# Half slots store each column half by itself, and the split of w1's last row moves to the next slot's head

## The chip, the cores and the metric

One core of a Trainium2 chip runs the whole program. The metric is the device time of one execution in microseconds. The core's engines are PE (matrix products, with PEld loading weights), DVE (vector), ACT (scalar), POOL (GpSimd) and SP (which issues most loads). Each engine takes its instructions in order from a queue of its own. Loads and stores with an index per row (indirect DMAs) are issued by POOL.

## The reference

Attention with a sigmoid in place of the softmax, then a mixture of eight experts in which each token goes to the one expert with the largest gate:

```python
scores = scale * q @ k.T - log(S)          # 8 batches, 12 heads, S = 448, head_dim = 64
attn   = sigmoid(scores);  x = attn @ v    # x: 3584 tokens x 768
logits = x @ w_gate                        # 8 experts
e_idx  = argmax(logits);  gate_w = softmax(logits)[e_idx];  eom = sigmoid(x @ w_output_gate)
for e in range(8):
    h = relu(x[mask_e] @ w1[e])            # 768 -> 1024
    out[mask_e] = gate_w * eom[:, e] * (h @ w2[e])    # 1024 -> 768
```

## The kernel before

Attention fills the first part of the span. `route` finds each token's expert and scatters one line per token (row numbers, token number, factor) into a list in DRAM, ordered by expert. The experts' part then works in slots. A slot takes up to 256 tokens of one expert: POOL gathers their rows of x (`gather`, L501), DVE transposes them (`turn_x`, L558), ACT and DVE split x and the weights into a rounded high part and the remaining low part (`split`, L532 and L533; pairs of w1 rows in `split_w1`, L536 and L539), PE forms both layers from the parts, ACT scales the result into `y` (`layer2_out`, L621), and POOL scatters y's rows into `out` (L623). The tokens left over per expert go into wide slots (192 tokens, whose last 64 go out by `layer2_q`, L677) and half slots (128 tokens). How many there are depends on the data: the last loops are nested `tc.If` blocks, one block a slot. In the profiled execution three wide slots and two half slots run; the half slots are the last 45 us.

A half slot `half_slot(j, y)` works for itself and prepares its successor, whether or not one will run (there are eight blocks): it asks for the successor's w1 and w2 (issued only if the expert changes), gathers the successor's rows, waits for POOL to drain (L717), forms its layer 1, then turns the successor's x, splits w1's first four rows and x (`split_w1(0)`, `split_x`, `split_w1(1)`), and, while PE forms layer 2, row 4 of w1 (`split_w1_row(4)`). Then each column half n of the output is evicted by ACT. After that row 5 of w1 is split. The order of the work on each engine is the order of the program (a manual schedule). What the engines wait for is worked out by the framework from the regions that instructions write and read; the text writes no wait by hand.

`out` is written by every slot. A slot's store is an indirect DMA with one index per token, of 768 words a row. `layer2_q` sees `out` as twice as many rows of 384 words, with its own index list `ltq` (twice the token's number, plus the half). `finish` stores a slot's second half late, inside the next slot; in half slot 0 it is the last wide slot's. `y` is one of two buffers, and half slot j uses `ys[j % 2]`. The half slots' index and factor are in `ltb`, eight lists of 128 tokens, filled once in `spread_rest`'s neighbourhood early in the experts' part. `ltb` lies in the tail of the buffer `gl1`, of which the last sixteen words are free.

Of the kernel before, what the change touches and what calls it, by code (L numbers as in the profile page):

```python
# [14 lines left out]
ALU = mybir.AluOpType  # L15
# [5 lines left out]
B, H, S, D = 8, 12, 448, 64  # L21
NPAIR = H // 2
E = 8
DM = H * D
DF = 1024
NT = B * S
# [28 lines left out]
def r32(ap):  # L55
    return ap.bitcast(F32)


class Kernel:
# [78 lines left out]
    def constants(self):  # L138
        nc = self.nc
# [21 lines left out]
            t, pattern=pattern, base=base, channel_multiplier=0, allow_small_or_imprecise_dtypes=True)  # L161
# [40 lines left out]
        own = gl[1].bitcast(I32)  # L202
# [11 lines left out]
        self.ltb = own[:, a:a + 2 * E].rearrange("p (k h w) -> p k h w", h=1, w=2)  # L214
        a += 2 * E
        self.at = own[0:GT, a:a + LGR + 1]
        self.route_tiles()

    def row_words(self):
# [260 lines left out]
    def spread_rest(self):  # L480
        g = self.nc.gpsimd
        a = EARLY + LATE_F
        for i in range(4):
            r, q = slice(32 * i, 32 * i + 32), slice(32 * (i % 2), 32 * (i % 2) + 32)
            own = self.lts[q, a:, 1]
            g.tensor_scalar(self.ltq[r, :, 0], own[:, :, 0], 2.0, float(i // 2), ALU.mult, ALU.add)
            g.tensor_copy(r32(self.ltq[r, :, 1]), r32(own[:, :, 1]))

    def load_rows(self, i):
        self.nc.gpsimd.indirect_dma_start(  # L490
            out=self.lr[i], out_offset=None, in_=self.lst.rearrange("(r t) w -> r (t w)", t=32),
            in_offset=bass.IndirectOffsetOnAxis(ap=self.at[:, i:i + 1], axis=0))
# [122 lines left out]
    def finish(self):  # L615
        self.layer2_out(self.psy[2], dict(lt=self.due.unsqueeze(1)), 0, 1, self.ys[1])

    def layer2_out(self, ps, s, t, n, y):
        nc = self.nc
        c = slice(384 * n, 384 * n + 384)  # L620
        nc.scalar.activation(y[:, c], ps, AF.Copy, scale=r32(s["lt"][:, t, 1:2]))  # L621
        if n == 1:
            nc.gpsimd.indirect_dma_start(  # L623
                out=self.out, out_offset=bass.IndirectOffsetOnAxis(ap=s["lt"][:, t, 0:1], axis=0),
                in_=y, in_offset=None, bounds_check=NT - 1, oob_is_err=False)
# [43 lines left out]
    def layer2_q(self, s, y):  # L669
        nc = self.nc  # L670
        ps = self.psy[0]
        for f in range(8):
            for n in range(2):
                nc.tensor.matmul(ps[64 * n:64 * n + 64], self.hq[:, f], self.w2r[:, f, 384 * n:384 * n + 384],
                                 start=(f == 0), stop=(f == 7))
        nc.scalar.activation(y[:, 0:384], ps, AF.Copy, scale=r32(s["lq"][:, 1:2]))
        nc.gpsimd.indirect_dma_start(  # L677
            out=self.out.rearrange("t (n c) -> (t n) c", n=2),
            out_offset=bass.IndirectOffsetOnAxis(ap=s["lq"][:, 0:1], axis=0),
            in_=y[:, 0:384], in_offset=None, bounds_check=2 * NT - 1, oob_is_err=False)  # L680

    def wide_slot(self, j):
        cur = self.wide_lists(j)
# [25 lines left out]
    def half_slot(self, j, y):  # L709
        nc = self.nc  # L710
        nx = None
        if j + 1 < E:
            nx = self.load_slot(self.tab_b, j + 1, self.half_lists(j + 1))
        if j:
            if nx is not None:
                self.gather(self.half_lists(j + 1))
            nc.gpsimd.drain()  # L717
        (wh, wl), (xh, xl), (hh, hl) = self.w1s, self.xs, self.hs

        def turn(n):  # L720
            ps = self.take("x", self.psx).rearrange("p a (b t) -> p (a b) t", b=2)
            for i in range(4):
                nc.tensor.transpose(ps[:, i], self.hb[:, 128 * (4 * n + i):128 * (4 * n + i + 1)], self.ident)  # L723
            fs = slice(4 * n, 4 * n + 4)
            self.split(ps, hh[:, fs, 0:HS], hl[:, fs, 0:HS])

        w2 = [self.w2_rows(k) for k in range(4)]
        low = lambda k: nc.vector.tensor_tensor(w2[k][2], w2[k][0], r32(w2[k][1]), ALU.subtract)
        for n in range(2):
            c = slice(512 * n, 512 * n + 512)  # L730
            ps = self.take("h", self.psh)
            for d in range(6):
                if n == 1 and d == 3:
                    turn(0)
                    low(2)
                    nc.scalar.copy(w2[3][1], w2[3][0])
                    low(3)
                nc.tensor.matmul(ps, xh[:, d, 0:HS], wh[d][:, c], start=(d == 0), stop=False)  # L738
                nc.tensor.matmul(ps, xh[:, d, 0:HS], wl[d][:, c], start=False, stop=False)  # L739
                nc.tensor.matmul(ps, xl[:, d, 0:HS], wh[d][:, c], start=False, stop=(d == 5))  # L740
            if n == 0:
                self.split_w2(0)
                self.split_w2(1)
            nc.scalar.activation(self.hb[:, c], ps, AF.Relu)
            if n == 0:
                nc.scalar.copy(w2[2][1], w2[2][0])
        cur = dict(lt=self.ltb[:, j])
        pss = self.psy[0:2]
        self.layer2_mm(pss[0], 0, 0, range(2))
        turn(1)  # L750
        if j == 0:
            self.finish()
        if nx is not None:
            self.turn_x(nx)
            self.split_w1(0)
            for k in range(3):
                self.split_x(nx, k)
            self.split_w1(1)
        self.layer2_mm(pss[0], 0, 0, range(2, 4))
        self.layer2_mm(pss[1], 0, 1, range(4))  # L760
        self.load_w2(nx)
        if nx is not None:
            self.split_w1_row(4)
        for n in range(2):
            self.layer2_mm(pss[n], 0, n, range(4, 8))
            self.layer2_out(pss[n], cur, 0, n, y)
        if nx is not None:
            self.split_w1_row(5)

    def attention(self, pool, rows):  # L770
        nc = self.nc
# [276 lines left out]
```

## Time and profile before

| | |
|---|---|
| time, median of 3 runs | 783.53 us (783.46 to 785.43) |
| the profiled execution | 785.01 us, of which the span from first to last instruction is 783.3 us |
| granted clock of TensorE, mean | 0.996 |
| busy: PE, DVE, ACT, POOL | 98%, 64%, 62%, 45% of the span |
| half slot 0, layer 1 on PE begins | 738.76 us |
| half slot 1, layer 1 on PE begins | 758.16 us |
| PE's last matmul ends | 775.98 us |

Times in the views are microseconds from the span's start. The busy shares are averages over the whole span; the change touches the last 45 us and an early line of the list's arithmetic. In a timeline a row is an instruction or a run of equal ones; the bracket at its end gives the engine's idle time before it and what ended that. A DMA row on POOL is the time in which POOL writes the transfer's descriptors; the landing, when the data is there, comes later.

### The profile page before, as it was taken

To read this page: it belongs to the slowest core of one execution; us is meant where nothing else is said; L and a number is where in the kernel's file an instruction comes from. 1 tells how busy PE (TensorE), PEld (TensorE's weight loads), DVE (VectorE), ACT (ScalarE), POOL (GpSimd) and SP (SyncE) were. 2 spreads that over 40 slices of the span, in tenths; PEclk is the share of its full clock that TensorE was granted. 3 is DMA by queue.
4 is the path that set the end of the run, shared out by engine and by line. 5 is a ranking of instruction groups with operands and counts; after the bars stand their busy time and mean duration, and the time that the engine had idled before them with its cause. 6 is when DMAs were issued, how large, how long until landed. Compare 5 with 4: busy or idle time off the path is not lost. (4 is left out here: it accounts for less than half of the span.)

```text
span 783.3 us, 15087 instructions
## 1 busy us (share of the span) xinstructions
PE 767.6 (98%) x5724; PEld 561.6 (72%) x5724; DVE 497.8 (64%) x800; ACT 488.1 (62%) x662; POOL 353.9 (45%) x464
## 2 busy tenths in 40 slices
PE   9999999999999999999999999999999999999896
PEld 4333433333443369899999989999899999889685
DVE  2334444443456768876786576858577685787677
ACT  5666666666668757565675565746556474675585
POOL 4003301230331676778895667255372643633522
PEclk9999999999999999999999999999999999999999
DMA  6352544445258550147666497511156655856771
GB/s 252 142 212 91 195 165 173 159 143 213 81 204 303 191 184 12 53 176 238 232 201 249 160 343 280 182 51 42 40 223 204 259 158 210 315 212 237 278 307 46
DMA packets 37616, 145.23 MB, mean 185 GB/s; under 512 B 5639, under 2 KB 7791, under 8 KB 33552
## 3 DMA queue, kind: packets, MB, share of 16 engines
q1 hardware_dynamic: 27696, 119.56, 42.6%
q0 software_dynamic: 9824, 24.46, 9.3%
q8 instruction: 51, 0.84, 0.4%
q14 instruction: 45, 0.37, 0.2%
HBM read 152.61 MB, written 23.05 MB: 224 GB/s over the span
## 5 line engine op out<-in xcount | busy, mean ns | idle before, releaser
L800 ACT ACTIVATE a<-ps,bias_s 128x896 f32<-128x896 f32 x168 | 169.1, 1008 | 96.6 <-PE ps L798 96.6
L576 PE MATMUL ps<-rounded 128*128 128x512 f32 (+1 forms) x672 | 225.9, 386 | 1.7 <-PEq L990 1.2
L501 POOL DMA_INDIRECT plain<-x_dram,lxs x122 | 181.9, 1491 | 65.2 <-issue 40.5
L577 PE MATMUL ps<-rounded 128*128 128x256 f32 (+1 forms) x672 | 184.1, 274 | 1.4 <-DVE rounded L539 1.2
L798 PE MATMUL ps<-kqv 64*64 64x448 f32 x1344 | 157.9, 541 | 0.4 <-ACT a L800 0.4
L807 PE MATMUL ps<-a,kqv 64*64 64x448 f32 x1344 | 156.8, 536 | 0.0
L601 PE MATMUL ps<-w2h,h 128*128 128x384 f32 x432 | 144.9, 335 | 0.0
L533 DVE TENSOR_TENSOR w2l<-plain,w2h 128x1536 fp32r<-128x1536 f32 x60 | 105.2, 1757 | 62.0 <-ACT w2h L532 61.4
L602 PE MATMUL ps<-w2l,h 128*128 128x384 f32 x432 | 144.4, 334 | 0.0
L603 PE MATMUL ps<-w2h,h 128*128 128x384 f32 x432 | 144.4, 334 | 0.0
L576 PEld LDWEIGHTS ps<-rounded 128*128 128x128 f32 x672 | 125.8, 187 | 25.0 <-issue 3.0
L577 PEld LDWEIGHTS ps<-rounded 128*128 128x128 f32 x672 | 127.2, 189 | 2.3 <-DVE rounded L539 2.0
L807 PEld LDWEIGHTS ps<-a,kqv 64*64 64x64 f32 x1344 | 51.6, 133 | 75.3 <-issue 74.2
L539 DVE TENSOR_TENSOR rounded<-plain,rounded 128x2048 fp32r<-128x2048 f32 x46 | 103.3, 2284 | 1.8 <-ACT rounded L536 1.8
L798 PEld LDWEIGHTS ps<-kqv 64*64 64x64 f32 x1344 | 48.7, 133 | 74.0 <-issue 60.7
L532 ACT CAST w2h<-plain 128x1536 fp32r<-128x1536 f32 x60 | 88.1, 1472 | 19.3 <-PEq L995 6.3
L584 ACT COPY gl<-ps 128x256 f32<-128x256 f32 (+1 forms) x112 | 40.3, 360 | 93.9 <-PE ps L577 87.0
L536 ACT CAST rounded<-plain 128x2048 fp32r<-128x2048 f32 x46 | 87.3, 1903 | 0.0
L601 PEld LDWEIGHTS ps<-w2h,h 128*128 128x128 f32 x432 | 81.1, 188 | 2.3 <-issue 1.8
L602 PEld LDWEIGHTS ps<-w2l,h 128*128 128x128 f32 x432 | 81.1, 188 | 0.1
L603 PEld LDWEIGHTS ps<-w2h,h 128*128 128x128 f32 x432 | 81.1, 188 | 0.0
L623 POOL DMA_INDIRECT out<-y,due x11 | 18.3, 1666 | 117.6 <-ACT gl L584 92.4
(209 smaller groups left out, 716.5 us busy)
## 6 DMA issues: line engine op xcount, KB each, us to landing
plain<-w SPq DMA_DIRECT2D x68, 768.0 KB
plain<-w SPq DMA_DIRECT2D x48, 1024.0 KB
kqv<-kqv SPq DMA_DIRECT2D x23, 1344.0 KB
x_dram<-xt SPq DMA_DIRECT2D x8, 1344.0 KB
plain<-w SPq DMA_DIRECT2D x6, 512.0 KB
plain<-x_dram,lxs POOLq DMA_INDIRECT x122, 5.0
kqv<-kqv SPq DMA_DIRECT2D x1, 896.0 KB
lst<-plain POOLq DMA_DIRECT2D x1, 726.0 KB, 7.2
```

The lines of the kernel that those rows point to most:

```text
L501: self.nc.gpsimd.indirect_dma_start(out=s["xg"][:, g], out_offset=None, in_=x4, in_offset=bass.IndirectOffsetOnAxis(ap=s["lx"][:, g:g + 1] ...
L532: self.nc.scalar.copy(hi, raw)
L533: self.nc.vector.tensor_tensor(lo, raw, r32(hi), ALU.subtract)
L539: self.nc.vector.tensor_tensor(self.w1p[1][k], self.w1r[:, 2 * k:2 * k + 2], r32(self.w1p[0][k]), ALU.subtract)
L576: nc.tensor.matmul(out, wh[d][:, c], both, start=(d == 0), stop=False)
L577: nc.tensor.matmul(ps[:, 0:n], wl[d][:, c], self.xc[:, d, 0, 0:n], start=False, stop=(d == 5))
L601: nc.tensor.matmul(ps, hh[:, f, tk], wh, start=(f == 0), stop=False)
L602: nc.tensor.matmul(ps, hh[:, f, tk], wl, start=False, stop=False)
L603: nc.tensor.matmul(ps, hl[:, f, tk], wh, start=False, stop=(f == 7))
L798: nc.tensor.matmul(ps[half[h], j, 0:S], kg[half[j], e, 0, o:o + 64], kg[half[j], e, 1], start=True, stop=True)
L800: nc.scalar.activation(at[u % 4], ps[:, :, 0:S], AF.Sigmoid, bias=self.bias_s, scale=1.0 / math.sqrt(D))
L807: nc.tensor.matmul(self.ps_o[e][h][half[j], 0:S], v[half[h], 6 if i == 3 else 3 * e + c, j], a[half[h], j], start=(i in ((0, 3 if h else 4 ...
```

## The change

`spread_rest` computes a second index list `ltc` for the half slots, with two entries per token: twice the token's number, plus 0 and plus 1. `layer2_out` takes it as `rows` from `half_slot` and then stores each column half by itself, right behind its eviction, by the helper `store_part` that `layer2_q` uses too. So a half slot issues two indirect stores of 384-word rows instead of one of 768-word rows. And `split_w1_row(5)` is no longer the last thing of a half slot but the first thing of the next one, inside its block.

```diff
@@ (the lists)
+        self.ltc = own[:, S - 2 * E:].rearrange("p (k w) -> p k w", w=2)
@@ spread_rest
+        for n in range(2):
+            g.tensor_scalar(self.ltc[:, :, n:n + 1], self.ltb[:, :, :, 0], 2.0, float(n), ALU.mult, ALU.add)
@@ layer2_out
-    def layer2_out(self, ps, s, t, n, y):
+    def layer2_out(self, ps, s, t, n, y, rows=None):
         nc = self.nc
         c = slice(384 * n, 384 * n + 384)
         nc.scalar.activation(y[:, c], ps, AF.Copy, scale=r32(s["lt"][:, t, 1:2]))
-        if n == 1:
+        if rows is not None:
+            self.store_part(rows[:, n:n + 1], y[:, c])
+        elif n == 1:
             nc.gpsimd.indirect_dma_start(
                 out=self.out, out_offset=bass.IndirectOffsetOnAxis(ap=s["lt"][:, t, 0:1], axis=0),
                 in_=y, in_offset=None, bounds_check=NT - 1, oob_is_err=False)
@@ layer2_q, and the new helper
-        nc.gpsimd.indirect_dma_start(
+        self.store_part(s["lq"][:, 0:1], y[:, 0:384])
+
+    def store_part(self, rows, y):
+        self.nc.gpsimd.indirect_dma_start(
             out=self.out.rearrange("t (n c) -> (t n) c", n=2),
-            out_offset=bass.IndirectOffsetOnAxis(ap=s["lq"][:, 0:1], axis=0),
-            in_=y[:, 0:384], in_offset=None, bounds_check=2 * NT - 1, oob_is_err=False)
+            out_offset=bass.IndirectOffsetOnAxis(ap=rows, axis=0),
+            in_=y, in_offset=None, bounds_check=2 * NT - 1, oob_is_err=False)
@@ half_slot, head
         nx = None
+        if j:
+            self.split_w1_row(5)
         if j + 1 < E:
             nx = self.load_slot(self.tab_b, j + 1, self.half_lists(j + 1))
@@ half_slot, end
         for n in range(2):
             self.layer2_mm(pss[n], 0, n, range(4, 8))
-            self.layer2_out(pss[n], cur, 0, n, y)
-        if nx is not None:
-            self.split_w1_row(5)
+            self.layer2_out(pss[n], cur, 0, n, y, self.ltc[:, j])
```

## Rows read from the trace of the kernel before

**Rows 1.** Windows: busy us of PE, PEld, DVE, ACT, POOL; clock, DMA share, GB/s.

```profile
776.00:778.00 2.00, 0.00 (x0) 0.00 (x0) 2.00 (x2) 1.83 (x3) 0.83 (x1) 1.00 0.05 16
781.50:783.30 1.80, 0.00 (x0) 0.00 (x0) 0.00 (x0) 0.00 (x0) 0.00 (x0) 0.50 0.00 0
```

**Rows 2.** Source view of L1003 from 781 us: duration (ns), first and last start.

```profile
L1003 POOLq INC_SWDGE_SEM  x1: 188/188/188, 781.5 to 781.5; - x1
```

**Rows 3.** Timeline of POOL, half slots: start, us, what, idle time before and releaser.

```profile
752.45 0.99 POOL L623 DMA_INDIRECT out<-y,due  x1 [14.79 <-ACT y L621]
760.45 1.03 POOL L623 DMA_INDIRECT out<-y,gl  x1 [7.01 <-ACT rounded L532]
761.79 2.51 POOL L501 DMA_INDIRECT plain<-x_dram,gl  x1 [0.30 <-DVE rounded L533]
764.61 1.35 POOL L501 DMA_INDIRECT plain<-x_dram,gl  x1 [0.30 <-issue]
766.25 0.95 POOL L501 DMA_INDIRECT plain<-x_dram,gl  x1 [0.30 <-issue]
767.51 1.46 POOL L501 DMA_INDIRECT plain<-x_dram,gl  x1 [0.30 <-issue]
777.17 1.17 POOL L623 DMA_INDIRECT out<-y,gl  x1 [8.21 <-ACT y L621]
```

**Rows 4.** Timeline of ACT, the half slots.

```profile
757.54 0.58 ACT L621 ACTIVATE y<-ps,gl 128x384 f32<-128x384 f32 x1
...
772.16 1.02 ACT L532 CAST rounded<-plain 128x256 fp32r<-128x256 f32 x3 [1.01 <-DVE plain L558]
...
775.85 1.04 ACT L621 ACTIVATE y<-ps,gl 128x384 f32<-128x384 f32 x2
776.78 1.04 ACT L532 CAST rounded<-plain 128x1024 fp32r<-128x1024 f32 x1
```

**Rows 5.** Timeline of DVE, the half slots.

```profile
759.42 2.35 DVE L533 TENSOR_TENSOR rounded<-plain,rounded 128x1024 fp32r<-128x1024 f32 x2
761.69 3.42 DVE L533 TENSOR_TENSOR w2l<-plain,w2h 128x1536 fp32r<-128x1536 f32 x2
...
766.39 3.41 DVE L728 TENSOR_TENSOR w2l<-plain,w2h 128x1536 fp32r<-128x1536 f32 x2
...
771.09 0.98 DVE L558 STREAM_TRANSPOSE plain<-plain 128x768 f32<-128x768 f32 x1 [0.69 <-DMA plain<-x_dram,gl]
...
775.17 2.28 DVE L539 TENSOR_TENSOR rounded<-plain,rounded 128x2048 fp32r<-128x2048 f32 x1
777.37 2.35 DVE L533 TENSOR_TENSOR rounded<-plain,rounded 128x1024 fp32r<-128x1024 f32 x2
```

**Rows 6.** Source view of L623, 752 to 753 us: a queue's wait (ns), landing.

```profile
L623 POOLq EVENT_SEMAPHORE  x1: 7428/7428/7428, 752.3 to 752.3; - x1
...
DMA to landing us min/median/max: 7.2/7.2/7.2
```

**Rows 7.** Timeline of POOL in a full slot: two stores in a row.

```profile
330.72 1.10 POOL L623 DMA_INDIRECT out<-y,lts  x1 [0.30 <-issue]
335.26 1.14 POOL L623 DMA_INDIRECT out<-y,lts  x1 [3.44 <-ACT h L589]
```

**Rows 8.** Source view of L623, 330 to 331 us: landing of the first.

```profile
DMA to landing us min/median/max: 3.7/3.7/3.7
```

**Rows 9.** Waits of the whole span: the scatters into the list.

```profile
POOL lst L317 <- DMA lst<-meta,posi: 41.3, 22, 5.3
```

**Rows 10.** Source view of L623 over the whole span: landing of its stores.

```profile
DMA to landing us min/median/max: 3.0/4.3/8.0
```

**Rows 11.** DMA view, 758 to 766 us: rate in 40 slices.

```profile
GB/s 277 200 169 61 77 61 31 15 15 0 0 0 0 0 0 0 0 0 0 0 461 399 338 369 384 0 0 0 0 0 0 82 0 0 0 230 154 38 31 31
```

**Rows 12.** Source view of L677, whole span: landing, rows of 384 words.

```profile
DMA to landing us min/median/max: 3.7/6.0/6.1
```

**Rows 13.** Source view of L486: index arithmetic on POOL, ns min/median/max.

```profile
L486 POOL TENSOR_SCALAR gl<-lts x4: 199/200/208, 417.4 to 418.7; 32x10 int32<-32x10 int32 x4
```

## The prediction

> **What bounds the kernel now.** I read the page first: PE is busy 98% of the span, so time can only be won or lost where PE is not the last to finish. The windows of the tail show such a place: from 776 us on PE does nothing, while DVE, ACT and POOL still work, and in the last 1.8 us no engine is busy [rows 1]. The span ends 1.8 us after POOL's queue gets past 781.5, and what it stands behind there is the landing of the last store: issued at 777.17, landed 4.3 us later [rows 2, 3]. So the end is set by one store, plus 1.8 us of closing work.
>
> Then I followed that store back through the timelines, each row giving what ended the idle time before it. The store starts 0.28 us after ACT's second eviction (776.89) [rows 3, 4]. The evictions start at 775.85, behind casts for a successor slot that never runs, and these start at 772.16, when DVE has turned x, for which DVE waited until 771.09 on the last gather [rows 4, 5]. That gather was issued at 767.51 as the last of four, the first at 761.79, right behind the store of half slot 0 at 760.45 [rows 3]. So the critical chain of the last slot begins at POOL in slot 0: store, four gathers, turn, casts, evictions, store, end. Whatever is put on POOL between 760 and 768 us, or between two stores, can reach the end.
>
> One wait in that chain decides the rest. The store at 760.45 was not waiting for its data: its first half had been evicted from 757.54 to 758.12 and its second shortly after [rows 4]. POOL's queue sat 7.43 us in one wait from 752.3, that is until 759.7; the store before it (`finish`, issued at 752.45, another y buffer) took 7.2 us to land, until 759.65, and 0.8 us later the next store started [rows 3, 6]. What these two share is `out`. The same stands at the two stores of a full slot: the first, issued at 330.72, lands 3.7 us later at 334.42, the second starts at 335.26, 0.84 us after that [rows 7, 8]. The scatters into the list behave so too: 22 times one waited for the landing of the one before, 41.3 us in all [rows 9]. I read this as a rule of this program: a store into `out` starts about 0.8 us after the previous store into `out` has landed.
>
> **Part 1, the index list.** Two POOL instructions in `spread_rest`, at most 0.2 us each by their neighbour of the same kind [rows 13], 340 us before the half slots and behind nothing that PE waits for: 0. Without that cover 0.4 us.
>
> **Part 2, two stores in half slot 0.** The first half (A) still starts at 760.45, since it waits for `finish`, not for its data. It lands 2.5 to 3.0 us after its start: the shortest landing of a whole store is 3.0 [rows 10], and in the store at 760.45 the bytes move for 1.0 us (five slices at 338 to 461 GB/s) [rows 11], half of which may go with half the bytes. Among gathers and weight loads the stores of 384-word rows took 3.7 to 6.1 [rows 12]; the half slots issue few loads, so I keep 3.7 as the slow end. So A lands at 763.0 to 763.5 and the second half (B) starts 0.8 us later, at 763.8 to 764.3. B is new on POOL, and the four gathers are queued behind it.
>
> What B takes depends on DVE. A gather that starts while DVE works on a pair of SBUF tensors ends only 0.85 to 0.9 us after that DVE instruction's end: the one at 761.79 took 2.51 and ended at 764.30, 0.9 after the first of the two w2 instructions (761.69, 3.42 for both) must have ended; the one at 764.61 ended 0.85 after the second; the store at 777.17 ended at 778.34, 0.89 after the DVE row that ended at 777.45. The gather at 766.25, started just before a DVE pair, took 0.95 [rows 3, 5]. So B, started inside the second w2 instruction (to 765.11), ends at 765.96. The gathers follow 0.30 us apart: the first from 766.26 to 767.21, the second 767.51 to 768.97 (where the fourth stood before), the third from 769.27, held until DVE's pair ends at 769.80, to 770.66, the fourth from 770.96 to 771.91, now without a DVE instruction in the way. Before, the turn began 2.12 us after the fourth gather's issue ended (768.97 to 771.09), so it now begins at 774.03: later by 2.9. If B is not held, the row of gathers comes one place earlier and the shift is 1.7; if B misses its place by a gather, 4.2. I take 2.9, since B's start falls well inside that DVE instruction.
>
> By the Trainium skill, SBUF — State Buffer, section "SBUF: two separate sides", DVE and GpSimd share a port pair as an exclusive lock, and the loser is blocked for the whole instruction; that is the shape of the 2.51 beside the 0.95. Without such a lock, with 0.95 for each of the five, the shift would be 1.0 instead of 2.9.
>
> **Part 3, two stores in the last slot.** Turn, casts and evictions stand in the same order on ACT and DVE, so the evictions end 2.9 us later, the first at 779.4 (776.43 before), the second at 779.8. They come back to back, so storing A early gains 0.46 us and no more. A starts at 779.65. DVE's w1 row then runs to 780.4, so A's issue ends at 781.25, and A lands 1.5 to 2.0 us later (2.5 to 3.0 less 1.0 of issue), at 783.0. B starts 0.8 us later, at 783.8. DVE has no more work by then, as the row-5 split is gone (below), so B issues in 1.0 and lands between 2.5 us (nothing in its way, half the bytes) and 4.3 (as the last store of before) after its start; I take the middle, 3.4: 787.2. With the closing 1.8 us the span ends at 789.0, that is 5.7 later than 783.3. The ends of this: shift 1.7 and quick landings, 3.4; shift 4.2, A landing 2.7 us after its issue (3.7 less 1.0) and B 4.3 after its start, 8.8.
>
> By the Trainium skill, DMA: Bandwidth & Descriptors, section "Anatomy of one DMA — SWDGE (gpsimd) path", a DMA costs about 2.0 us fixed plus its bytes at 436 GB/s. That is an estimate of 2.9 us for the whole store (3.0 in the trace, so it agrees) and of 2.45 for a half, which no trace here shows; two halves in a row then cost 2.0 us more than one whole before any wait is added, and with it the end would come 0.1 to 1.2 us earlier than in my sum.
>
> **Part 4, the move of row 5.** Between slots 0 and 1 nothing changes in order: ACT's cast and DVE's subtraction follow the evictions and precede the next slot's w2 parts in both kernels. The first gather was released by DVE's row 5 at 761.77 [rows 3, 5]; that release may now come at row 4, 1.2 us earlier, but POOL is then still in its stores, so it is worth 0. In the last slot the split vanishes, as no block follows: ACT 1.04 us and DVE 1.2 us [rows 4, 5], both beside the store's landing: DVE ended at 779.7, the landing came at 781.5. Worth 0, and without that cover 1.2 at most. Loads on SP are asked for in the same order.
>
> **Sum.** 0 + 2.9 (the gathers) + 2.8 (store behind store at the end) + 0 = 5.7 us, made in a profiled execution of 785.01 us, which is 1.5 above the median of 783.53. Carried to the median: 789.2 us.
>
> **Rivals.** (1) The halves do not wait for each other: the framework sees that they touch different halves of `out`. For it: the two index lists never meet. Against it: full stores never meet either, being of different tokens, and do wait. Then in slot 0 B starts at 761.79, is held by DVE to 764.3, and the gathers take the next places, 764.61 to 770.66: shift 1.7. At the end B is 0.3 us behind A, and the landing comes at about 783.5: in all 1.3 to 2.9, or 785.5 us. (2) Not slower: B goes out in 1.0 us at 761.79, without a wait and without being held. Then the gathers fall back into the places that they had, the shift is 0, and the last half, with half the bytes, lands 0.4 to 1.0 us earlier than the whole did: 782.8 us. It decides where B's issue ends before 763.1. The row at 761.79, which started there and took 2.51, speaks against it. (3) The split is made but hidden, because something else ends the span, such as DVE's tail: 783.5 us. Against it: the last idle 1.8 us follow the landing, not DVE.
>
> **Chances.** My forecast 0.81, rival (1) 0.11, (2) and (3) together 0.06, and 0.02 for anything faster that I do not see. A measurement of this kernel can tell 0.3%, 2.35 us, from no change. My forecast lies wholly above that, of rival (1) a third, and the rest is within: slower 0.85, the same 0.12, faster 0.03. The range takes the forecast's ends (786.9 to 792.3) and reaches down to the upper part of rival (1): 786.0 to 792.5.
>
> **What would show it.** In the changed kernel's timeline of POOL: two stores in slot 0, the first still at about 760.4, the second 3.3 to 3.8 us behind it and not 1.3; the first gather at about 766 instead of 761.8; the turn at 774 instead of 771.1; in the last slot two stores some 4 us apart; the queue's last step 1.8 us before the end. DVE's last instruction would end before the first half lands. If the second store follows the first by 1.3 us, the wait is not there and rival (1) or (2) holds; if the gathers start late but the turn does not, my account of DVE holding POOL is wrong.

## The result: slower by 0.8%, by 0.6% in a later set, with the profile after

The changed kernel takes 790.06 us in the median of 7 runs (788.44 to 794.77), the kernel before 784.25 us in as many (783.46 to 786.89). The ratio is 1.0081 with a 95% interval of 1.0057 to 1.0105. Eight more runs in a later set, in which the kernel before took 787.59 us, gave 1.0064 (1.0042 to 1.0086). The profiled execution took 789.21 us, its span is 787.5 us.

The answer to [rows 3] is POOL's timeline of the changed kernel in the half slots (start, length, what, idle time before it and its releaser). L628 is the store of the last wide slot, L685 the half stores, L504 the gathers:

```profile
751.66 0.98 POOL L628 DMA_INDIRECT out<-y,due  x1 [14.30 <-ACT y L624]
759.54 1.15 POOL L685 DMA_INDIRECT out<-y,gl  x1 [6.90 <-ACT rounded L535]
763.11 2.06 POOL L685 DMA_INDIRECT out<-y,gl  x1 [2.42 <-ACT hb L754]
765.48 0.99 POOL L504 DMA_INDIRECT plain<-x_dram,gl  x1 [0.31 <-issue]
766.77 1.40 POOL L504 DMA_INDIRECT plain<-x_dram,gl  x1 [0.30 <-issue]
768.47 1.33 POOL L504 DMA_INDIRECT plain<-x_dram,gl  x1 [0.30 <-issue]
770.11 0.95 POOL L504 DMA_INDIRECT plain<-x_dram,gl  x1 [0.30 <-issue]
778.84 1.65 POOL L685 DMA_INDIRECT out<-y,gl  x1 [7.78 <-ACT y L624]
782.91 0.99 POOL L685 DMA_INDIRECT out<-y,gl  x1 [2.42 <-DMA out<-y,gl]
```

Two stores stand where one stood, 3.57 us apart in slot 0 and 4.07 us apart in the last slot. The last bracket names what the second half waited for: the DMA that writes `out`. The bracket of the store at 763.11 names an ACT instruction (`hb`); a wait for several semaphores is put down to whichever came last. In a run below in which the second half goes elsewhere (its second profile), the second half starts 0.86 us before that instruction does, so that instruction is not what it waits for. So the wait is read from the landings. The source view of L685 in a window around single stores gives them:

```profile
DMA to landing us min/median/max: 2.7/2.7/2.7
```

The first half, issued at 759.54, has landed at 762.2, and the second starts 0.9 us after that, as full stores did [rows 6 to 8]. The last half lands 2.6 us after its start:

```profile
DMA to landing us min/median/max: 2.6/2.6/2.6
```

DVE's timeline answers to [rows 5]: the idle time before the turn (L561) has grown from 0.69 to 3.67 us, and row 4 is now the last thing that DVE does.

```profile
760.90 3.42 DVE L536 TENSOR_TENSOR w2l<-plain,w2h 128x1536 fp32r<-128x1536 f32 x2
...
773.25 0.98 DVE L561 STREAM_TRANSPOSE plain<-plain 128x768 f32<-128x768 f32 x1 [3.67 <-DMA plain<-x_dram,gl]
...
777.32 2.29 DVE L542 TENSOR_TENSOR rounded<-plain,rounded 128x2048 fp32r<-128x2048 f32 x1
779.52 1.22 DVE L536 TENSOR_TENSOR rounded<-plain,rounded 128x1024 fp32r<-128x1024 f32 x1
```

ACT's timeline answers to [rows 4]: the casts wait 3.99 us for the turn, and the evictions (L624) come late with them.

```profile
774.32 1.02 ACT L535 CAST rounded<-plain 128x256 fp32r<-128x256 f32 x3 [3.99 <-DVE plain L561]
...
777.99 1.04 ACT L624 ACTIVATE y<-ps,gl 128x384 f32<-128x384 f32 x2
```

And POOL's last step in the branch, the answer to [rows 2], again 1.8 us before the end of the span:

```profile
L1011 POOLq INC_SWDGE_SEM  x1: 213/213/213, 785.7 to 785.7; - x1
```

The half slots did not begin at the same time in the two profiled executions (the store of the last wide slot stands at 752.45 before and at 751.66 after; in later runs anywhere from 751 to 756, by set of runs and execution, in work that no edit here touches). So I count from that store. Before, the turn comes 771.09 - 752.45 = 18.64 us after it and the span's end 783.3 - 752.45 = 30.85. After: 773.25 - 751.66 = 21.59 and 787.5 - 751.66 = 35.84. The turn is 2.95 us later, the end 5.0.

### The profile page after: what moved, and what is told of

It reads as the page before. It is cut to its first block, busy times and chain, and to the rows that moved or that the text cites. A ratio compares the mean times of both kernels' runs of the same rounds, so it can differ in the third digit from the quotient of the medians.

```text
span 787.5 us, 15091 instructions
## 1 busy us (share of the span) xinstructions
PE 767.0 (97%) x5724; PEld 561.3 (71%) x5724; DVE 497.1 (63%) x799; ACT 487.0 (62%) x661; POOL 355.7 (45%) x468
## 5 line engine op out<-in xcount | busy, mean ns | idle before, releaser
L504 POOL DMA_INDIRECT plain<-x_dram,lxs x122 | 180.3, 1478 | 65.1 <-issue 39.2
L628 POOL DMA_INDIRECT out<-y,due x11 | 18.3, 1664 | 117.7 <-ACT gl L587 93.0
```

The costliest lines, as they stand in the source:

```text
L504: self.nc.gpsimd.indirect_dma_start(out=s["xg"][:, g], out_offset=None, in_=x4, in_offset=bass.IndirectOffsetOnAxis(ap=s["lx"][:, g:g + 1] ...
```

## Experiments

The theory: a store into `out` waits for the landing of the previous one. In slot 0 that delays the gathers behind the second half, and through turn, casts and evictions the last store; in the last slot it puts two landings in a row. The rivals: row 5's move takes part; the extra issue on POOL costs, and not the wait; the delay does not reach the end through the gathers. The table gives each kernel's times by the count above, from its own profile, and the ratio of its times to those of the kernel before in the same set of runs. Each end is that of one profiled execution, and the last store's landing alone moved it by up to 1 us, so differences of ends under 1 us decide nothing by themselves.

| kernel | last wide slot's store | turn after it | end after it | ratio (95%) |
|---|---|---|---|---|
| before | 752.45 | 18.64 | 30.85 | 1 |
| after | 751.66 | 21.59 | 35.84 | 1.0081 (1.0057 to 1.0105) |
| after, again | 753.26 | 21.56 | 35.84 | 1.0064 (1.0042 to 1.0086) |
| row 5 moved, whole stores | 751.92 | 18.69 | 30.08 | 0.9984 (0.9967 to 1.0001) |
| halves, row 5 not moved | 753.25 | 21.67 | 37.05 | 1.0080 (1.0051 to 1.0109) |
| halves in slot 0 alone | 751.17 | 21.60 | 32.83 | 1.0027 (1.0009 to 1.0046) |
| halves in the last slot alone | 751.89 | 18.63 | 32.81 | 1.0026 (1.0008 to 1.0043) |
| second half elsewhere, first profile | 751.88 | 23.86 | 36.0 | 1.0019 (1.0003 to 1.0034) |
| second half elsewhere, second profile | 756.48 | 20.25 | 32.4 | one run, 790.58 us |
| after, without the gather | 751.55 | 17.88 | 32.45 | 1.0015 (0.9998 to 1.0032) |
| before, gather moved ahead | 752.75 | 17.85 | 30.75 | 0.9983 (0.9970 to 0.9996) |
| the same, row 5 moved | 756.25 | 17.85 | 30.35 | 0.9998 (0.9982 to 1.0014) |
| the same, rows 4 and 5 moved | 754.25 | 18.36 | 30.05 | 0.9982 (0.9968 to 0.9996) |

**The two edits apart.** First the kernel before with row 5 at the next slot's head and whole stores:

```diff
         nx = None
+        if j:
+            self.split_w1_row(5)
...
-        if nx is not None:
-            self.split_w1_row(5)
```

> The kernel before with only w1's row 5 moved to the next half slot's head; each half slot still issues one whole store. My theory (the halves' stores wait for each other, and that is all that costs): within 0.3 us of before in the profile's half slots, ratio 1.000. In slot 0 the store starts 0.8 us after the landing of the one before, the first gather 1.3 us after it, the turn of the successor's x about 51.8 us after... that is 18.6 us after the store of the last wide slot's second half, as before. Rival A (the move of row 5 takes part in the loss, because ACT or DVE now meet it at the slot's head): +1 to +3 us, ratio 1.002 to 1.004. Rival B (the move is a gain that the split hides): -0.7 to -1.2 us, DVE ending before the last store's issue.

The turn stands where it stood (18.69 against 18.64). The end is 0.8 us earlier in the profile, because the last store landed 3.5 us after its start instead of 4.3; up to the end of that store's issue nothing is gained (25.94 us after the reference store, 25.89 before). The ratio's interval holds 1, so the times show no gain, and they exclude a loss of rival A's size: rival A falls. The profile's 0.8 us is rival B's forecast, so rival B stays open here. Then the halves with row 5 left at its old place:

```diff
-        if j:
-            self.split_w1_row(5)
...
             self.layer2_out(pss[n], cur, 0, n, y, self.ltc[:, j])
+        if nx is not None:
+            self.split_w1_row(5)
```

> The changed kernel with row 5 back at the end of the slot before; the two halves are stored one by one. My theory: the whole loss is here, +5 us like the changed kernel (ratio 1.006 to 1.009), first half to second half 3.6 us in slot 0 and about 4 us in the last slot, turn 2.9 us later than before against the last wide slot's store. Row 5's subtraction runs again at the end of the last slot but ends before the second half's issue, so it adds 0 to 0.4 us. Rival A (row 5's move takes part): +3 us or less. Rival B (the move was a gain of about 1 us inside the changed kernel): +6 us.

The ratio is that of the changed kernel, so, as far as the intervals tell, the whole loss comes from storing in halves. In this execution the end is 6.2 us late, over the 5 of the theory, and the last slot shows where: the second half waits 3.60 us for the first one's DMA, 1.2 more than in the changed kernel.

```profile
780.50 1.65 POOL L685 DMA_INDIRECT out<-y,gl  x1 [7.84 <-ACT y L624]
785.75 0.99 POOL L685 DMA_INDIRECT out<-y,gl  x1 [3.60 <-DMA out<-y,gl]
```

The first half took 4.4 us to land here (source view of L685), against 3.3 in the changed kernel. A wait for a landing hands on whatever that landing happened to take.

The 6 us are again rival B's forecast, and the late landings are not spread at random. In all three profiles with row 5 at the end of the last slot (before, this one, and the gather moved ahead below) the first or only store there landed 2.6 to 3.2 us after the end of its issue. In the others whole stores took 2.2 to 2.4 us and first halves 1.6 to 2.0. The DMA packets of the three traces show where the delay sits: a packet of 8 KB of the instruction queue (q14) runs amid the store's, some of the store's packets follow only at its end, and of the store's sixteen closing packets of 4 bytes the last comes 0.4 to 1.1 us after the fifteenth. In the other traces no q14 packet starts between the first and the last of that store's packets of data, and the last closing packet is behind by 0.3 us or less. So in the profiles the move of row 5 is worth something: 0.8 us with whole stores, 1.2 with halves, 0.4 with the gather moved ahead. The times do not show it (1.0080 without the move, 1.0081 with it), and that the place of row 5 is what brings the q14 packet there was not tested. The DMA view of before from 778.9 to 780 us has that packet beside the store's (queue and kind: packets, MB, share of the 16 engines):

```profile
q0 software_dynamic: 73, 0.37, 88.5%
q14 instruction: 1, 0.01, 4.1%
```

**One slot at a time.**

```diff
-            self.layer2_out(pss[n], cur, 0, n, y, self.ltc[:, j])
+            self.layer2_out(pss[n], cur, 0, n, y, None if j % 2 else self.ltc[:, j])
```

> The changed kernel, but only half slots with an even number store their halves one by one; of the two that run here that is the first. My theory: the loss of part 2 alone. The turn in the last slot is 2.9 us later than before against the last wide slot's store, and the last (whole) store and the end too: +2.9 us, ratio 1.0037. Rival (only the tail of the last slot costs, what happens in slot 0 is hidden): the turn may be late but the end is within 0.5 us of before.

The turn is 2.96 us late (21.60), as expected. The end is only 2.0 us late, since the last store, whole again, landed 3.3 us after its start and not 4.3 as in the profile of before. The ratio 1.0027 is 2.1 us, and its interval holds the expected 1.0037. Against the profile with row 5 moved and whole stores, whose last landing was not late, it is 2.7 us late. The rival, that slot 0's part is hidden, falls. The opposite choice:

```diff
+            self.layer2_out(pss[n], cur, 0, n, y, self.ltc[:, j] if j % 2 else None)
```

> The changed kernel, but only half slots with an odd number store their halves one by one; of the two that run here that is the last. My theory: the loss of part 3 alone. Gathers and turn stand as before; in the last slot the second half starts 0.8 us after the first has landed, some 4 us after its start, and the end comes 1.8 to 2.8 us later: ratio 1.0025 to 1.0035. With the 2.9 of the first slot it adds up to the changed kernel's. Rival (the tail absorbs the second store, the loss is all in the gathers): the end is within 0.5 us of before.

The turn is where it was before (18.63) and the end 2.0 us late, with the two stores 3.55 us apart, the second again released by the first one's DMA:

```profile
776.66 1.10 POOL L685 DMA_INDIRECT out<-y,gl  x1 [8.27 <-ACT y L624]
780.21 1.00 POOL L685 DMA_INDIRECT out<-y,gl  x1 [2.45 <-DMA out<-y,gl]
```

Both parts cost about 2 us each in the times, 1.0027 and 1.0026. Their sum, 1.0053, is to be set beside the changed kernel, run once more:

> The changed kernel once more, to set the two one-slot runs (ratios 1.0027 and 1.0026) beside the whole on one chip. Theory: the parts add, ratio 1.005 to 1.0075, the profile's end 5 us later against the last wide slot's store. Rival (the parts together cost more than their sum, by something that needs both): 1.008 or more.

The one-slot runs were made in an earlier set on another chip, so each ratio is to the kernel before of its own set. It gave 1.0064 (1.0042 to 1.0086), which holds the sum; the first measurement's interval starts at 1.0057. That the parts cost a little more together is neither shown nor excluded. The profile's end is 35.84 us after the reference store, as in the first profile.

**The wait, with the issue kept.** The second half goes to a tensor of its own.

```diff
+        self.spare = dram.tile([2 * NT, 384], F32, name="spare")
...
-            self.store_part(rows[:, n:n + 1], y[:, c])
+            self.store_part(rows[:, n:n + 1], y[:, c], self.spare if n else None)
```

> The changed kernel, but the second column half of each half slot is stored into a spare DRAM tensor of the same shape instead of out (those output columns are left out). The same number of stores, rows and bytes; only the reason to wait for the first half is gone. My theory (the wait costs, not the extra store): the second half starts 0.3 us after the first one's issue ends, in slot 0 it is held by VectorE to about 2.5 us, the turn is 1.7 us later than before, and in all the end is 1.3 to 2.9 us later, ratio 1.002 to 1.004, some 3 us faster than the changed kernel. Rival (the extra issue and its descriptors cost, whether it waits or not): as slow as the changed kernel, ratio 1.006 to 1.010. Rival 2 of the prediction (the second half is not held, everything falls back into its place): -0.4 to -1.0 us.

The times agree with the lower end of the theory: 785.77 us, ratio 1.0019, an interval that excludes the changed kernel's 1.006 and over. The profile did not. POOL's timeline in slot 0:

```profile
760.05 5.35 POOL L686 DMA_INDIRECT out<-y,gl  x1 [7.17 <-ACT rounded L536]
765.71 0.98 POOL L686 DMA_INDIRECT spare<-y,gl  x1 [0.30 <-issue]
766.99 1.46 POOL L505 DMA_INDIRECT plain<-x_dram,gl  x1 [0.30 <-issue]
```

The second half does start 0.30 us after the first, without a wait. But the first half's issue lasted 5.35 us and pushed everything back. DVE at that time:

```profile
758.86 2.36 DVE L537 TENSOR_TENSOR rounded<-plain,rounded 128x1024 fp32r<-128x1024 f32 x2
761.13 3.42 DVE L537 TENSOR_TENSOR w2l<-plain,w2h 128x1536 fp32r<-128x1536 f32 x2
```

The issue began as the second row instruction did (the two rows take 2.36 us from 758.86) and ended 0.85 us after the second w2 instruction, at 764.55: it was held through three DVE instructions, not one. The profiled execution took 789.57 us, the slowest of the twelve, whose median is 785.77. So the same kernel was profiled once more:

> The run with the second half stored into a spare tensor (those output columns left out) once more, for a second look: in its first profile the first half's issue in slot 0 took 5.35 us, through three DVE instructions in a row, and the turn came 5.2 us late, while its times were 1.5 us above before. Theory (whether POOL gets its turn between two DVE instructions is chance): here the first half takes 1.0 to 1.2 us and the second about 2.5, turn 1.7 us late. Rival (the wait that was removed had kept the first half out of DVE's way in every execution): again above 5 us.

```profile
764.24 1.28 POOL L686 DMA_INDIRECT out<-y,gl  x1 [6.76 <-ACT rounded L536]
765.82 2.50 POOL L686 DMA_INDIRECT spare<-y,gl  x1 [0.30 <-issue]
768.62 1.38 POOL L505 DMA_INDIRECT plain<-x_dram,gl  x1 [0.30 <-issue]
```

DVE's two row instructions there, and its turn:

```profile
763.45 2.35 DVE L537 TENSOR_TENSOR rounded<-plain,rounded 128x1024 fp32r<-128x1024 f32 x2
...
776.73 0.98 DVE L562 STREAM_TRANSPOSE plain<-plain 128x768 f32<-128x768 f32 x1 [2.31 <-DMA plain<-x_dram,gl]
```

Here the first half takes 1.28 us, the second 2.50, the turn is 1.6 us late and the end 1.57: the sum that the prediction gave for its rival (1), mechanism for mechanism. So of the 5.0 us in the changed kernel's profile the extra issue, held by DVE, costs 1.6, and the wait the other 3.4; this rests on one profile each. The times say the same within their intervals: 1.5 us of the 5.0 to 6.4 that the two ratios of the changed kernel make. The long hold is not a property of the program, by these two profiles of it. What decides it was not shown; they differ in where the issue begins, in the first as one row instruction gives way to the next, in the second in the middle of one.

**The way to the end.** The changed kernel without the half slots' gather:

```diff
         if j:
-            if nx is not None:
-                self.gather(self.half_lists(j + 1))
             nc.gpsimd.drain()
```

> The changed kernel without the half slots' own gathers (in this data the one that runs fetches rows for a slot that never runs). My theory: the stores of slot 0 reach the end only through the gathers behind them, so the shift of 2.9 us goes, and the turn falls to where DVE is free, 0.7 us earlier than before; what is left is the last slot's two stores: +1.1 to +2.1 us against before, ratio 1.0015 to 1.0027. Rival (the turn is late for another reason, such as DVE or ACT order, and the gathers only stand beside it): still +5 us.

```profile
769.43 0.97 DVE L561 STREAM_TRANSPOSE plain<-plain 128x768 f32<-128x768 f32 x1
```

The turn falls from 21.59 to 17.88, where DVE is free (no idle time stands before it), though both halves of slot 0 are stored as late as in the changed kernel (759.63 and 763.03). So they reach the turn through the gathers alone. The end is 1.6 us late: the last slot's pair, less what the earlier turn gives back. The ratio, 1.0015, agrees, but its interval holds 1.

**Ahead of the store.** If the gathers hang on the stores in front of them, they can go in front:

```diff
             self.turn_x(nx)
+            if j == 0:
+                self.gather(self.half_lists(2))
...
-            if nx is not None:
+            if nx is not None and j > 1:
                 self.gather(self.half_lists(j + 1))
```

> The kernel before, with the gather that half slot 1 issues at its head moved into half slot 0, right behind the turn that frees its buffer, so that it stands ahead of slot 0's store on POOL and does not wait for the landing of the store before. My theory of the chain (store, gathers, turn, casts, evictions, last store): the turn starts where DVE is free, 0.7 us earlier, and the end comes 0.3 to 0.7 us earlier: ratio 0.9991 to 0.9996, which the times can hardly tell but the profile can. Rival (the gathers are not on the chain): no change of the turn. If the store of slot 0 now waits behind the gathers, it is late by up to 5 us without harm.

```profile
770.60 0.97 DVE L558 STREAM_TRANSPOSE plain<-plain 128x768 f32<-128x768 f32 x1
```

The turn is 0.8 us earlier (17.85) and no longer waits for a DMA. The ratio is 0.9983, its interval 0.9970 to 0.9996: by the times this beats the kernel before, and with it the changed one. In the profile the end gains only 0.1 us, since the last store's issue was held by DVE, 1.81 us, ending 0.9 us after row 4's subtraction:

```profile
763.19 1.43 POOL L623 DMA_INDIRECT out<-y,gl  x1 [0.30 <-ACT w2h L532]
777.15 1.81 POOL L623 DMA_INDIRECT out<-y,gl  x1 [12.53 <-ACT y L621]
```

So two more versions take DVE's work away from beside that store, by moving row 5, or rows 4 and 5, to the next slot's head:

```diff
         nx = None
+        if j:
+            self.split_w1_row(4)
+            self.split_w1_row(5)
```

> A candidate: whole stores as before, the gather of half slot 1 issued in slot 0 ahead of its store (as in the run with the moved gather), and row 5's split at the next slot's head as in the change. My theory: turn 0.8 us earlier against the last wide slot's store, second eviction bound by PE's end, no row-5 work beside the last store: end 0.5 to 1.5 us earlier than before, ratio 0.998 to 0.9994. Rival (the last store's landing, 3.3 to 4.5 us after its start in the profiles so far, hides it): 1.000.

> As the candidate before it, but rows 4 and 5 are both split at the next slot's head, so that in the last slot DVE has no weight row left when the last store is issued. My theory (a store on POOL is held while DVE works on two SBUF tensors): the last store issues in 1.0 us instead of 1.2 to 1.8 and the end comes 0.8 us earlier still; in slot 1 the rows come up to 0.5 us later for PE, which costs up to that: ratio 0.9975 to 0.9992. Rival (the rows come too late for PE in slot 1): 1.000 or above, with PE waiting for DVE at the first layer's last rows.

With row 5 alone the store is held as before (1.80 us) and the ratio is 0.9998. No gain can be seen, not even the 0.9983 of the moved gather alone, which was timed in an earlier set of runs; the intervals overlap, and whether that gain is real stays open. With both rows the store issues in 0.99 us, though the turn comes 0.5 us later than with the moved gather alone, because DVE gets the rows late:

```profile
764.05 1.00 POOL L623 DMA_INDIRECT out<-y,gl  x1 [0.30 <-ACT w2h L532]
779.16 0.99 POOL L623 DMA_INDIRECT out<-y,gl  x1 [14.11 <-ACT y L621]
```

Its ratio is 0.9982 (0.9968 to 0.9996), some 1.4 us. The end is 0.8 us earlier in the profile, but not by the shorter issue: against the reference store that issue ends at 25.90 us, before at 25.89, and the 0.8 us is the landing after it, 2.3 us instead of 3.2. So the times say that this version beats the kernel before, by little, and the profile does not show how. Three of the versions tried have ratios of 0.998; which of them gains stays open.

## Why the prediction was right

The direction, the cause and the size held: 789.2 us forecast and 790.06 measured. Of +5.7 us forecast, the medians measured +5.8 and, in the later set, +4.3, the ratios 6.4 and 5.0, and the profile 5.0. That the first medians hit the forecast to a tenth is luck: a term of the sum was off by 0.8 us, and the times spread by more than that.

- The store behind the landing: forecast 0.8 us after it; measured 0.8 to 0.9 in slot 0 and in the last slot. The runs with the second half elsewhere show that the shared tensor is the reason: the same issue, the same bytes, no wait.
- The first half's landing: forecast 2.5 to 3.0; measured 2.7.
- The second half held by DVE in slot 0: forecast to end 0.85 us after the second w2 instruction; measured 763.11 + 2.06 = 765.17, and that DVE pair ended at 764.32.
- The gathers: forecast 0.95, 1.46, 1.39 and 0.95 us; measured 0.99, 1.40, 1.33 and 0.95. The turn: forecast 2.9 us late, measured 2.95.
- The last slot: the first half's issue held by DVE, forecast 1.6, measured 1.65. Its landing and the 0.8 us came as forecast. The term that was mis-sized is the last landing: 3.4 us was the middle between 2.5 and the 4.3 of before, and it took 2.6. That makes the profile's 5.0 out of the forecast's 5.7. The 4.3 of before, which set the upper bound, was a late one, with row 5 still beside it; in the run with halves in slot 0 alone the last whole store landed in 3.3.
- The index list and the move of row 5 at nothing: two instructions of 0.2 us at 418.7 us, and a ratio of 0.9984 whose interval holds 1. In the profiles the move gains 0.4 to 1.2 us by the last slot's landings, which part 4 did not foresee; whether the times gain by it stays open.
- Rival (1) was not what the kernel does, but its sum (1.3 to 2.9 us) was what the kernel does when the shared tensor is taken away (1.57 in the profile, 1.5 in the times).

What is not explained is the spread of the times: three of the changed kernel's first seven runs lie at 792.6 to 794.8, and none of these was profiled. Three things seen here could make it: a late landing handed on by a wait (halves with row 5 not moved), an issue on POOL held several times (second half elsewhere, first profile), and the work ahead of the half slots, after which the reference store stood anywhere from 751 to 756 us. Which of them it is was not shown.

## What to carry to other kernels

Before a store is cut in two, look in the trace at what its predecessor on the same tensor makes it wait for. Where stores into one tensor wait for each other's landing, two halves cost a second landing and a second issue, and save only the time of half the bytes, here 0.4 us. And what is queued behind a store on its engine waits with it: look at the gathers that stand there, and put them in front if their data allow it.

## What the runs showed of the hardware

With nothing in the way a half store lands 2.6 us after a start whose issue takes 0.99, a whole one 3.0 [rows 10] with about the same issue: 0.4 us is all that half the bytes give. By the Trainium skill, DMA: Bandwidth & Descriptors, section "Anatomy of one DMA — SWDGE (gpsimd) path", the difference would be the 0.2 MB of a half at 436 GB/s, an estimate of 0.45 us, and the trace agrees.

A landing can also be late by what else the DMA engines carry: in the three traces named above an 8 KB packet of the instruction queue amid the store's packets goes with a last packet 0.4 to 1.1 us behind.

An issue on POOL that meets DVE can lose more than once: 5.35 us through three DVE instructions in one execution, 1.28 us in another of the same program. By the Trainium skill, SBUF — State Buffer, section "SBUF: two separate sides", whichever of the two starts first holds the port pair for its instruction; that fits the single holds (the 2.50 us, for one). The 5.35 us takes three of them in a row, with POOL waiting from before the last two DVE instructions began, and no run here shows why POOL did not get its turn between them.
